# Ten row stores and sixteen stores of encoded weights are issued from ScalarE's queue instead of SyncE's

## The chip, the core and the metric

The kernel runs on one core of a Trainium2 chip. Five engines have an instruction stream each: TensorE (PE, with its weight loads listed as PEld), VectorE (DVE), ScalarE (ACT), GpSimd (POOL) and SyncE (SP). The metric is the device time of one execution in microseconds (us), lower being better. SP issues nearly all transfers of the kernel before; its issues are listed as SPq, those of ScalarE as ACTq.

## The reference

```python
for t in range(S):                       # retention, B=4 H=8 S=768 D=64
    state = gamma * state + einsum('bhd,bhe->bhde', k[:, :, t], v[:, :, t])
    y[:, :, t] = scale * einsum('bhd,bhde->bhe', q[:, :, t], state)
x = y.transpose(0, 2, 1, 3).reshape(B * S, H * D)        # 3072 x 512
h = x @ w_in;  x = maximum(0.01 * h, h) @ w_out          # 512 -> 2048 -> 512
h = x @ w_in2; out = where(h > 0, h, exp(minimum(h, 0)) - 1) @ w_out2
```

The weights come as float64, and the matrix products are made in split fp32 (a high and a low half, three products each).

## The kernel before, in words

**Stages.** The retention is computed in 24 chunks of 128 tokens (six for each of four sequences). A first list schedule, not touched, covers chunks 0 to 13 and the first steps of the first network. A second list schedule covers the rest: chunks 14 to 23 beside the last old-style steps of the first network, then both networks in groups of seven products by a Strassen-like scheme. The order of PE's work is written out; the order on ACT, DVE, POOL and SP comes from a planner. It takes tasks with an engine, a cost, the tasks they depend on and a lag after their end, and places on each engine in turn the one that its model can start first. Every engine's stream is then run in that order.

**A chunk c (14 to 23).** PE makes the scores (`sc`, L262), DVE masks them (`pt`, L317), PE makes the outputs and state (`o`, L271 to L285), ACT copies the output rows out of PSUM into the tile `xs` (task `xs`, L293), and a transfer stores them into the DRAM scratch `xscr` (task `xso`, L289). There is one `xs` tile, so the copy of chunk c+1 waits until the store of chunk c has landed. DVE adds the state (`st`, L299, or L301 for a sequence's first chunk). The scores of the next chunk use the same PSUM bank, so they wait for `xs` and `st`. Between them PE makes a first product (L920) and a second product (L929) of the old-style steps. The rows of `xscr` are read back later for the products (L1187).

**Encoded weights i (0 to 7).** The high and low weights are added on DVE into two tiles `fe` (L1028, twice: tasks `fa` and `fb`), four differences go into a tile `te` (L1029 to L1032), ACT writes the high halves over the two `fe` tiles (`hi0`, `hi1`, L1040), DVE takes the low halves in `te` (L1041), and three transfers go into the DRAM scratch `w1enc`: `sh0` and `sh1` (L1042, from `fe`) and `sl` (L1044, from `te`). The two `fe` tiles are all there are, so the next `fa` and `fb` wait for the landing of `sh0` and `sh1`. The sum `fa` is also the last reader of a piece of the weights, and its end frees the room into which rows of `xscr` are loaded (tile `w`, L1187), which ACT then casts (L1173).

**Groups.** In a group, products 0 to 6 (L1242) go to PSUM banks; ACT copies three of them out (L1268), DVE adds others (L1276), and product 4 needs the second of those copies. The operands of the products are made from loaded rows by DVE (L1170), cast by ACT (L1173) and split by DVE (L1177).

Completion of transfers is counted on eight semaphores that all transfers take in turn, whichever engine issues them, so a transfer also waits for the one that had its semaphore before.

Of the kernel before, what the change touches and what calls it, by code (L numbers as in the profile page):

```python
# [33 lines left out]
C = 128  # L34
# [5 lines left out]
CPB = BLK // C  # L40
# [19 lines left out]
def body(ctx: ExitStack, tc: tile.TileContext, kkv, w1, w2, tabs, rows, out):  # L60
    nc = tc.nc
# [9 lines left out]
    xscr = {j: dp.tile([P, KD, BLK], F32, name=f"xscr{j}") for j in range(2, NB)}  # L71
    w1enc = [dp.tile([P, NPR, BLK], F32, name=f"w1enc{i}") for i in range(HM)]
# [96 lines left out]
    def conv_ops():  # L169
        yield c_put, pieces[0]  # L170
        for n, i in enumerate(pieces):
            yield c_exp, i
            yield c_bias, i
            if n:
                yield c_split, pieces[n - 1]
            yield c_top, i
            yield c_low, i
            yield c_sign, i
            if n + 1 < len(pieces):
                yield c_put, pieces[n + 1]  # L180
            yield c_mul, i
            yield c_cast, i
        yield c_split, pieces[-1]

    queue = list(conv_ops())
# [22 lines left out]
    with ExitStack() as actx:  # L208
# [16 lines left out]
        def prep_k(c):  # L225

            k = kv[c][:, 2, :].rearrange("p (h d) -> p h d", h=H)
            nc.gpsimd.tensor_tensor(k, k, ktab.unsqueeze(2).to_broadcast([P, H, D]), ALU.mult)

        def prep_q(c):  # L230

            nc.gpsimd.tensor_tensor(kv[c][:, 1, :], kv[c][:, 1, :], qtab, ALU.mult)
# [23 lines left out]
        def quarters(c, sc):  # L256

            for i in range(2):
                for x in range(2):
                    for k, r in HEADS:  # L260
                        a = (2 * i + k) * C + x * HC
                        nc.tensor.matmul(sc[half(k), r, cells(i, x)], kv[c][half(r), 0, a : a + HC], kv[c][half(r), 1, a : a + C - x * HC],  # L262
                                         start=True, stop=True, skip_group_check=True)
# [21 lines left out]
                            nc.tensor.matmul(o[p : p + n, k, pair(i)], st[half(r), 2 * k + i, z * n : (z + 1) * n], kv[c][half(r), 1, pair(2 * i + k)],  # L285
                                             start=False, stop=True, skip_group_check=True)

        def rows_out(c, x):
            nc.sync.dma_start(out=xscr[c // CPB][:, :, c % CPB * C : (c % CPB + 1) * C], in_=x)  # L289

        def rows_copy(o, x):
            y = o[:, :, : 2 * C].rearrange("p k (i t) -> p k i t", i=2)
            nc.scalar.copy(x.rearrange("p (k i) t -> p k i t", k=2), y)  # L293

        def state(c, o):
            n = st.rearrange("p (k i) d -> p k (i d)", k=2)
            m = sg.rearrange("p (k i) d -> p k (i d)", k=2)
            if c % NCB:
                nc.vector.tensor_tensor(n, m, o[:, :, 2 * C : 2 * C + 2 * D], ALU.add)  # L299
            else:  # L300
                nc.vector.tensor_copy(n, o[:, :, 2 * C : 2 * C + 2 * D])  # L301
# [4 lines left out]
        def chunk_tasks(c, task, pe_task, x_bank, t, x, needs, takes=None, uses=None, after=None):  # L306


            cb = c % NCB
            late = {"lag": 2.0} if takes else {}  # L310
            takes, uses = takes or {}, uses or {}

            def more(n):
                return dict(([("use", uses[n])] if n in uses else []) + ([("take", takes[n])] if n in takes else []))

            pe_task(("sc", c), 0.95, needs["sc"], lambda: quarters(c, x_bank()), **more("sc"))
            task(("pt", c), "V", 0.96, [("sc", c)] + needs["pt"], lambda: nc.vector.tensor_tensor(t()[:, :, : 2 * TRI], x_bank()[:, :, : 2 * TRI], steps_mask, ALU.mult), **more("pt"))  # L317
            ready = [("pt", c)]
            if cb < NCB - 1:
                task(("pk", c), "G", 1.05, needs["kv"], lambda: prep_k(c), **more("pk"))  # L320
                ready.append(("pk", c))
            if cb:
                task(("pq", c), "G", 1.3, [("sc", c)], lambda: prep_q(c), **more("pq"))
                ready += [("pq", c)] + needs["st"]
            yield
            pe_task(("o", c), 0.98 + (0.5 if cb < NCB - 1 else 0.0) + (0.67 if cb else 0.0), ready, lambda: outputs(c, x_bank(), t()), **more("o"))
            task(("xs", c), "A", 0.6, [("o", c)] + needs["xs"], lambda: rows_copy(x_bank(), x()), **more("xs"))
            task(("xso", c), "Q", 0.8, [("xs", c)], lambda: rows_out(c, x()), **late, **more("xso"))
            if cb < NCB - 1:
                task(("st", c), "V", 0.41, [("o", c)] + needs["sg"], lambda: state(c, x_bank()), **more("st"))  # L330
            if cb < NCB - 2:
                task(("sg", c), "V", 0.55, [("st", c)], lambda: decayed(c), **more("sg"))
# [466 lines left out]
        def task(key, eng, cost, deps, fn, use=(), take=None, lag=0.0):  # L799

            queued.update((key, d[1]) for d in deps if d is not None and d[0] == "queued")
            tasks[key] = eng, cost, [d[1] if d[0] == "queued" else d for d in deps if d is not None], fn, take, lag
            uses_of[key] = list(use) + ([take[1]] if take else [])
            for u in uses_of[key]:
                uses.setdefault(u, []).append(key)
            if eng == "P":
                pe.append(key)
# [93 lines left out]
        for k in range(2):  # L901
            f = lazy(lambda: cv.tile([P, 2, BLK], F32, tag="f", name="nt"))
# [53 lines left out]
        for s in range(N0, NS):  # L956
# [3 lines left out]
                 use=[("gf", s), ("gfs",)], take=("ghi", ("ghi", s)))  # L960
# [47 lines left out]
        def enc_tasks(i):  # L1008
            n = QB
            EA, EB, ET, U = ("ea", i), ("eb", i), ("et", i), ("encs",)  # L1010

            def enc(op, eng, cost, deps, fn, use=(), take=None, lag=0.0):
                task(("e", i, op), eng, cost, [("e", i, d) if isinstance(d, str) else d for d in deps], fn, list(use) + [U], take, lag)

            def whole(m):
                return lambda: (f32(wt[0, m, 0][:, :BLK]), f32(wt[0, m, 0][:, BLK:]))

            def tw(k):
                return at(ET)[:, k]

            def fa():
                return at(EA)

            def fb():
                return at(EB)

            for nm, m, key in (("fa", i, EA), ("fb", i + HM, EB)):
                enc(nm, "V", 0.69, [], lambda w=whole(m), key=key: tt(at(key), *w(), add), use=wa(m), take=("ef", key))  # L1028
            enc("t1", "V", 0.42, ["fa", "fb"], lambda: tt(tw(1), fb()[:, :n], fa()[:, :n], sub), use=[EA, EB], take=("pf", ET))  # L1029
            enc("t3", "V", 0.42, ["t1"], lambda: tt(tw(2), fb()[:, n:], fb()[:, :n], sub), use=[EB, ET])  # L1030
            enc("t2", "V", 0.42, ["t1"], lambda: tt(tw(0), fb()[:, n:], tw(1), sub), use=[EB, ET])
            enc("t4", "V", 0.42, ["t2"], lambda: tt(tw(3), fa()[:, n:], tw(0), sub), use=[EA, ET])  # L1032
            for k, key, before in ((0, EA, ["t2", "t4"]), (1, EB, ["t2", "t3", "t4"])):
                def hi(key=key):
                    return at(key).rearrange("p (b c) -> p b c", b=2)

                def t(k=k):
                    return at(ET)[:, 2 * k : 2 * k + 2]

                enc(f"hi{k}", "A", 0.62, before, lambda hi=hi, t=t: nc.scalar.copy(hi().bitcast(F32R), t()), use=[key, ET])  # L1040
                enc(f"lo{k}", "V", 0.7, [f"hi{k}"], lambda hi=hi, t=t: tt(t().bitcast(F32R), t(), hi(), sub), use=[key, ET])  # L1041
                enc(f"sh{k}", "Q", 0.8, [f"hi{k}"], lambda hi=hi, k=k: nc.sync.dma_start(out=w1enc[i][:, 2 + 2 * k : 4 + 2 * k, :n], in_=hi()),  # L1042
                    use=[key], lag=4.0)
            enc("sl", "Q", 0.9, ["lo0", "lo1"], lambda: nc.sync.dma_start(out=w1enc[i][:, 2:6, n:], in_=at(ET)), use=[ET], lag=4.0)  # L1044
            for k in (0, 1, 6):
                stored["e", i, k] = []
            for k in range(2, 6):
                stored["e", i, k] = [("e", i, f"sh{k // 2 - 1}"), ("e", i, "sl")]
# [130 lines left out]
        for q, (L, j) in enumerate(SBS):  # L1179
# [28 lines left out]
            for n in ("11", "12", "22", "s3", "s1", "s2", "s4"):  # L1208
                if n in loaded_by:
                    raw, known, use, take = raw_x(q, n), [loaded_by[n]], [X(n)], None  # L1210
                    free = [("mk", q, "s1")] if n == "22" else []
                else:
                    raw, key = (r3, T("3")) if n == "s3" else (rs, T("s"))
                    known, use, take = [("mk", q, n)], [key] + ([] if n == "s1" else [X(n)]), ("x", X(n)) if n == "s1" else None
# [240 lines left out]
        while able:  # L1455
            pick = {}
            for x, r in able.items():
# [7 lines left out]
                c = (max(r, free[eng]), begin(x))  # L1465
# [4 lines left out]
            eng, cost, _, fn, take, lag = tasks[x]  # L1470
# [108 lines left out]
```

## Time and profile before

| | us |
|---|---|
| median of 3 runs | 1092.84 (1091.79 to 1094.06) |
| the profiled execution | 1092.51 |
| its span | 1090.6 |
| PE busy in the span | 1075.7 (99%) |
| DVE busy | 821.7 (75%) |
| ACT busy | 669.1 (61%) |

The span runs from the first to the last instruction of the profiled execution; 1.9 us of its time lie around it. PE being busy in 99% of the span means that a change can gain little more than PE's idle time, and that whatever makes PE wait longer shows in full.

### The profile page before, as it was taken

The page shows a single profiled execution, that of the slowest core. Times are in us where ns is not written, and L with a number is a line of the kernel's source. Part 1 is how long each engine was busy: PE and PEld are TensorE (multiplying, and loading weights), DVE is VectorE, ACT ScalarE, POOL GpSimd, SP SyncE. Part 2 cuts the span into 40 slices and gives each one's busy share as a digit, 9 for nine tenths or more (in the row PEclk, how much of TensorE's full clock was granted, in tenths as well). Part 3 has the DMA queues.
Part 4 walks back from the last instruction along what each step waited for, and adds up shares of the span by engine and source line. Part 5 has one row for each costly group of instructions (what it writes and reads, how often), then busy time and mean ns, then how long its engine had stood idle before and what let it go on. Part 6 is the DMA issues. An engine that isn't in the chain of part 4 may idle for free.

```text
span 1090.6 us, 18038 instructions
## 1 busy us (share of the span) xinstructions
PE 1075.7 (99%) x6745; PEld 880.5 (81%) x6745; DVE 821.7 (75%) x1300; ACT 669.1 (61%) x1128; POOL 53.9 (5%) x45
## 2 busy tenths in 40 slices
PE   9999999989999999999999999999999999999998
PEld 6778787767888888888888888888888888888886
DVE  5999987776755776557775669989988889979942
ACT  4675552333655665455654478788888778878831
POOL 4111212220000000000000000000000000000000
PEclk9999999999999999999999999999999999999999
DMA  9975547979888877776877966786676776674473
GB/s 353 393 290 192 204 136 236 338 252 314 275 266 273 263 222 219 236 235 206 296 238 247 322 207 188 263 272 202 203 226 192 259 225 193 201 227 149 122 234 108
DMA packets 115600, 258.40 MB, mean 237 GB/s; under 512 B 10924, under 2 KB 41772, under 8 KB 111160
## 3 DMA queue, kind: packets, MB, share of 16 engines
q1 hardware_dynamic: 115488, 257.14, 72.0%
q8 instruction: 54, 0.88, 0.3%
q14 instruction: 34, 0.28, 0.1%
q10 hardware_dynamic: 24, 0.09, 0.0%
HBM read 200.57 MB, written 56.62 MB: 236 GB/s over the span
## 4 chain that ended last, share of the span: by engine, by line
PE 91%; DMA 4%; DVE 4%; issue 1%; ACT 0%; SPq 0%; DVEq 0%; ACTq 0%
PE y L1354 40%; PE x L1242 15%; PE h L1242 10%; PE px L1242 10%; PE h L199 5%; PE y L609 4%; PE y L929 2%; DMA w1enc<-fe 1%; DMA xscr<-xs 1%; PE px L920 1%; DMA kv<-in_kkv 1%; PE x L262 1%; PE x L271 1%; PE x L285 0%; DMA w<-xscr 0%
## 5 line engine op out<-in xcount | busy, mean ns | idle before, releaser
L1354 PE MATMUL y<-w,ghi 128*128 128x512 f32 x768 | 236.4, 389 | 0.0
L1354 PE MATMUL y<-ghi,w 128*128 128x512 f32 x512 | 177.0, 389 | 0.0
L1354 PEld LDWEIGHTS y<-w,ghi 128*128 128x128 f32 x768 | 144.0, 188 | 30.0 <-ACT gk L943 0.2
L1354 PE MATMUL y<-w,glo 128*128 128x512 f32 x384 | 149.4, 389 | 0.0
L1354 PEld LDWEIGHTS y<-ghi,w 128*128 128x128 f32 x512 | 96.1, 188 | 20.0
L1242 PE MATMUL x<-w 128*128 128x512 f32 x432 | 109.6, 389 | 0.0
L1374 DVE TENSOR_TENSOR glo<-gk,ghi 128x512 fp32r<-128x512 f32 x92 | 63.3, 689 | 49.4 <-ACT ghi L1371 48.7
L1354 PE MATMUL y<-glo,w 128*128 128x512 f32 x256 | 99.6, 389 | 0.0
L1242 PEld LDWEIGHTS x<-w 128*128 128x128 f32 x432 | 81.1, 188 | 16.8
L1371 ACT CAST ghi<-gk 128x512 fp32r<-128x512 f32 x92 | 57.0, 621 | 60.0 <-PE y L1354 57.8
L1276 DVE TENSOR_TENSOR gk<-gk,x 128x512 f32<-128x512 f32 x67 | 45.9, 686 | 51.5 <-PE x L1242 40.0
L1354 PEld LDWEIGHTS y<-w,glo 128*128 128x128 f32 x384 | 72.1, 188 | 15.1
L1323 DVE SCALAR_TENSOR_TENSOR a<-nt,a 128x512 f32<-128x512 f32 x96 | 65.9, 686 | 8.7 <-ACT nt L1319 8.5
L1331 DVE SCALAR_TENSOR_TENSOR nt<-a,nt 128x512 f32<-128x512 f32 x96 | 66.3, 691 | 2.7
L1327 DVE SCALAR_TENSOR_TENSOR nt<-nt 128x512 f32<-128x512 f32 x96 | 65.7, 685 | 0.0
L1311 ACT ACTIVATE nt<-nt 128x512 f32<-128x512 f32 x96 | 60.8, 633 | 2.7 <-DVE gk L1335 0.2
L1315 ACT ACTIVATE a<-nt 128x512 f32<-128x512 f32 x96 | 60.8, 633 | 2.2
L1242 PE MATMUL h<-w 128*128 128x512 f32 x240 | 60.9, 389 | 0.0
L1242 PE MATMUL px<-w 128*128 128x512 f32 x240 | 60.9, 389 | 0.0
L1319 ACT ACTIVATE nt<-nt 128x512 f32<-128x512 f32 x96 | 59.4, 620 | 0.0
L1354 PEld LDWEIGHTS y<-glo,w 128*128 128x128 f32 x256 | 48.0, 188 | 10.0
L199 PE MATMUL h<-xhi,w 128*128 128x512 f32 x168 | 55.3, 394 | 0.0
(205 smaller groups left out, 2048.4 us busy)
## 6 DMA issues: line engine op xcount, KB each, us to landing
w<-w2scr SPq DMA_DIRECT2D x96, 512.0 KB, 4.0
w<-w1scr SPq DMA_DIRECT2D x168, 256.0 KB, 3.4
w<-w1enc SPq DMA_DIRECT2D x112, 256.0 KB, 3.9
kv<-in_kkv SPq DMA_DIRECT2D x22, 1024.0 KB, 7.5
raw<-in_w SPq DMA_DIRECT2D x40, 512.0 KB, 5.3
raw<-in_w SPq DMA_DIRECT2D x12, 1024.0 KB, 9.5
w2scr<-raw SPq DMA_DIRECT2D x16, 512.0 KB, 4.3
w1enc<-w SPq DMA_DIRECT2D x24, 256.0 KB, 3.9
```

The source lines that it names most:

```text
L199: nc.tensor.matmul(h, a, x, start=(n == 0), stop=(n == 3 * KD - 1))
L1242: nc.tensor.matmul(to, a, x, start=(first and z == 0), stop=(z == 5), skip_group_check=True)
L1276: task(("s", *hk[b]), "V", 0.7, [("c", *hk[b])] + deps, lambda: tt(at(t), at(t), bank[name], add), use=[t])
L1311: nc.scalar.activation(t, n, AF.Tanh, scale=-0.5)
L1315: nc.scalar.activation(a, t, AF.Copy, bias=-0.5, scale=0.5)
L1319: nc.scalar.activation(n, n, AF.Exp, scale=-1.0)
L1323: nc.vector.scalar_tensor_tensor(out=a, in0=n, scalar=1.0, in1=a, op0=ALU.add, op1=ALU.mult)
L1327: nc.vector.scalar_tensor_tensor(out=t, in0=n, scalar=1.0, in1=t, op0=ALU.add, op1=ALU.mult)
L1331: nc.vector.scalar_tensor_tensor(out=t, in0=a, scalar=2.0, in1=t, op0=ALU.add, op1=ALU.mult)
L1354: nc.tensor.matmul(ybank[d], a, x, start=(first and n == 0), stop=(last and n == 2))
L1371: task(hi, "A", 0.62, [made_by, last_hi[0]], lambda h=h, hi=hi: nc.scalar.copy(at(hi), at(h)), use=[h], take=("ghi", hi))
L1374: task(lo, "V", 0.7, [hi], lambda h=h, hi=hi, lo=lo: tt(at(lo), at(h), f32(at(hi)), sub), use=[h, hi], take=("glo", lo))
```

## The change

Sixteen stores of `fe` tiles (`sh0`, `sh1` of i = 0 to 7) and the ten stores of rows of chunks 14 to 23 are issued by ACT, from its own queue, where SP issued them. For the planner they become tasks of ACT of 0.5 us each, with lags of 5.0 and 5.5 us (before: 0.8 us of SP, lags of 4.0 and 2.0 us). The order of ACT, DVE and SP in the second list schedule comes out differently everywhere; the order of PE and POOL is the same. The transfers keep their sizes and addresses.

```diff
-        def rows_out(c, x):
-            nc.sync.dma_start(out=xscr[c // CPB][:, :, c % CPB * C : (c % CPB + 1) * C], in_=x)
+        def rows_out(c, x, queue=nc.sync):
+            queue.dma_start(out=xscr[c // CPB][:, :, c % CPB * C : (c % CPB + 1) * C], in_=x)
...
-            late = {"lag": 2.0} if takes else {}
...
-            task(("xso", c), "Q", 0.8, [("xs", c)], lambda: rows_out(c, x()), **late, **more("xso"))
+            if takes:
+                task(("xso", c), "A", 0.5, [("xs", c)], lambda: rows_out(c, x(), nc.scalar), lag=5.5, **more("xso"))
+            else:
+                task(("xso", c), "Q", 0.8, [("xs", c)], lambda: rows_out(c, x()), **more("xso"))
...
-                enc(f"sh{k}", "Q", 0.8, [f"hi{k}"], lambda hi=hi, k=k: nc.sync.dma_start(out=w1enc[i][:, 2 + 2 * k : 4 + 2 * k, :n], in_=hi()),
-                    use=[key], lag=4.0)
+                enc(f"sh{k}", "A", 0.5, [f"hi{k}"], lambda hi=hi, k=k: nc.scalar.dma_start(out=w1enc[i][:, 2 + 2 * k : 4 + 2 * k, :n], in_=hi()),
+                    use=[key], lag=5.0)
```

Three places show what becomes of the order. Line numbers of the changed kernel are one lower (L316) or two higher than those of the kernel before.

ACT at chunk 17 and encoded weights 3, before, each row with the semaphores that it waits for (`xs` is the copied row tile, `gf` and `ghi` belong to the old-style steps):

```order
L293 COPY xs_2011<-x2_1891 128x512 [waits DMAHW5_49,DVE_49,PE_49]
L1040 CAST fe_1895<-te_1907 128x512 [waits DMAHW1_49,DVE_49]
L1040 CAST fe_1901<-te_1907 128x512 [waits DMAHW3_49]
L932 ACTIVATE gf_1931<-px_1890 128x512 [waits PE_49]
L959 CAST ghi_1772<-gf_1931 128x512 [waits Activation_49]
L293 COPY xs_2011<-x2_1891 128x512 [waits DMAHW4_49,DVE_49,PE_49]
```

The same place on ACT after the change:

```order
L293 COPY xs_2011<-x2_1891 128x512 [waits DMAHW5_49,DVE_49,PE_49]
L289 DMA xscr4_84<-xs_2011 512x1x128 [waits DMAHW1_49,Activation_49]
L1042 CAST fe_1895<-te_1907 128x512 [waits DVE_49]
L1042 CAST fe_1901<-te_1907 128x512 [waits DMAHW2_49]
L1044 DMA w1enc3_89<-fe_1895 128x2x256 [waits Activation_49]
L1044 DMA w1enc3_89<-fe_1901 128x2x256 [waits DMAHW4_49,Activation_49]
L934 ACTIVATE gf_1931<-px_1890 128x512 [waits PE_49]
L961 CAST ghi_1772<-gf_1931 128x512 [waits Activation_49]
L293 COPY xs_2011<-x2_1891 128x512 [waits DMAHW1_49,DVE_49,PE_49]
```

The row store stands directly behind its copy and the two stores directly behind their casts; the next activation stands behind all three issues.

DVE between the masks of chunk 18 and the encoded weights 4, before (`y0`, `y1` are sums of the old-style steps, `stg` the state):

```order
L317 TENSOR_TENSOR pt_137<-x2_1891,tab_134 128x2x384
L986 TENSOR_TENSOR ws_2160<-ws_2160,y0_1434 128x512 x2
L986 TENSOR_TENSOR ws_2321<-ws_2321,y1_1445 128x512 x2
L1028 TENSOR_TENSOR fe_1895<-w_846 128x512
L301 COPY stg_133<-x2_1891 128x256
L1028 TENSOR_TENSOR fe_1901<-w_1537 128x512
L1029 TENSOR_TENSOR te_1907<-fe_1901,fe_1895 128x256
```

The same place on DVE after the change:

```order
L316 TENSOR_TENSOR pt_137<-x2_1891,tab_134 128x2x384
L1030 TENSOR_TENSOR fe_1901<-w_846 128x512
L988 TENSOR_TENSOR ws_2155<-ws_2155,y0_1434 128x512 x2
L988 TENSOR_TENSOR ws_2321<-ws_2321,y1_1445 128x512
L301 COPY stg_133<-x2_1891 128x256
L988 TENSOR_TENSOR ws_2321<-ws_2321,y1_1445 128x512
L1030 TENSOR_TENSOR fe_1895<-w_1537 128x512
L1031 TENSOR_TENSOR te_1907<-fe_1895,fe_1901 128x256
```

The first encoding sum now stands ahead of the four sums, and takes the tile `fe_1901`, whose store is the second of the two; one of the four sums has moved behind the state copy. At encoded weights 5 the first encoding sum likewise takes the tile of the second store.

ACT at the first group of products, before (`px` is the bank of products 0, 2, 4 and 5; the cast of `xhi1_120` makes an operand of product 6):

```order
L1268 COPY gk_3022<-px_1890 128x512
L1295 ACTIVATE gk_3022<-gk_3022 128x512
L1268 COPY gk_3022<-px_1890 128x512
L1371 CAST ghi_1868<-gk_3022 128x512
L1173 CAST xhi1_120<-ws_2646 128x1024
L99 COPY e2_3064<-raw2_2992 128x512
L1268 COPY gk_3022<-px_1890 128x512
```

The same place on ACT after the change:

```order
L1270 COPY gf_1931<-px_1890 128x512
L99 COPY e2_3031<-raw2_2973 128x512
L1175 CAST xhi1_120<-ws_2646 128x1024
L1270 COPY gf_2042<-px_1890 128x512
L1297 ACTIVATE gf_1931<-gf_1931 128x512
L1373 CAST ghi_1868<-gf_1931 128x512
L106 ACTIVATE e2_3031<-e2_3031,ebias_118 128x512
L1270 COPY gk_3076<-px_1890 128x512
```

The second copy out of `px`, which releases product 4, has moved from ahead of the cast of `xhi1_120` to behind it.

## Rows read from the trace of the kernel before

**Rows 1.** The page, part 1: busy us, share of the span, instructions.

```profile
PE 1075.7 (99%) x6745; PEld 880.5 (81%) x6745; DVE 821.7 (75%) x1300; ACT 669.1 (61%) x1128; POOL 53.9 (5%) x45
```

**Rows 2.** Stretches: PE, PEld, DVE, ACT, POOL busy, granted clock, DMA share, GB/s.

```profile
230.00:240.00 10.00, 7.10 (x81) 5.48 (x83) 7.56 (x10) 1.22 (x2) 2.74 (x2) 0.83 0.76 247
...
164.00:262.00 98.00, 92.42 (x1450) 71.97 (x1449) 72.19 (x112) 32.36 (x53) 22.40 (x16) 0.98 0.85 279
262.00:1086.00 824.00, 824.00 (x3635) 681.72 (x3633) 609.16 (x990) 542.85 (x933) 0.00 (x0) 1.00 0.71 227
```

**Rows 3.** Timeline of PE, 205 to 262 us: start, duration, work [idle before it].

```profile
208.45 0.50 PE L920 MATMUL h<-xhi,w 128*128 128x512 f32 x1
...
212.33 0.90 PE L262 MATMUL x<-kv 64*64 64x128 f32 x32 [0.86 <-DVE stg L301]
...
216.82 0.90 PE L271 MATMUL x<-pt,kv 64*64 64x128 f32 x32 [0.64 <-DVE pt L317]
...
222.35 0.90 PE L262 MATMUL x<-kv 64*64 64x128 f32 x32 [0.60 <-DVE stg L299]
...
233.97 1.56 PE L262 MATMUL x<-kv 64*64 64x128 f32 x32 [2.90 <-DVE stg L299]
...
253.12 0.90 PE L262 MATMUL x<-kv 64*64 64x128 f32 x32 [0.26 <-DVE stg L299]
...
257.27 0.90 PE L271 MATMUL x<-pt,kv 64*64 64x128 f32 x32 [0.31 <-DVE pt L317]
```

**Rows 4.** The chain that ended last, 160 to 265 us: start, us, what.

```profile
201.64 0.42 DVE te L1032
...
203.22 0.63 ACT fe L1040
...
205.69 5.44 DMA xscr<-xs
...
211.23 0.59 ACT xs L293
...
211.85 0.04 DVE stg L301
...
216.24 3.73 DMA w1enc<-fe
...
220.07 0.70 DVE fe L1028
...
220.79 4.61 DMA w<-xscr
...
226.37 0.62 ACT fe L1040
...
227.01 4.83 DMA w1enc<-fe
```

**Rows 5.** Stores from the tile `fe`, 165 to 262 us: issue ns, then landing.

```profile
L1042 SPq DMA_DIRECT2D w1enc<-fe x16: 359/370/564, 170.5 to 257.5; - x16
...
DMA to landing us min/median/max: 2.1/4.6/5.7
```

**Rows 6.** Stores from the tile `xs`, same stretch.

```profile
L289 SPq DMA_DIRECT2D xscr<-xs x10: 525/525/1510, 175.8 to 261.3; - x10
```

**Rows 7.** Timelines of ACT and DVE, 160 to 262 us.

```profile
202.73 0.59 ACT L293 COPY xs<-x 128x512 f32<-128x512 f32 x1 [5.21 <-DMA xscr<-xs]
...
206.04 2.50 DVE L986 TENSOR_TENSOR ws<-ws,y 128x512 f32<-128x512 f32 x4
```

**Rows 8.** Timelines of SP, DVE and ACT at the first group of products.

```profile
262.57 0.45 SPq L1187 DMA_DIRECT2D xhi<-xscr  x1
...
270.06 1.22 DVE L1170 TENSOR_TENSOR ws<-xhi,ws 128x1024 f32<-128x1024 f32 x1 [1.43 <-DMA xhi<-xscr]
...
271.32 1.05 ACT L1173 CAST xhi<-ws 128x1024 fp32r<-128x1024 f32 x1 [0.98 <-DVE ws L1170]
```

**Rows 9.** Timeline of PE there: product 4, first group.

```profile
271.08 1.52 PE L1242 MATMUL px<-w 128*128 128x512 f32 x6
```

## The prediction

> **What bounds the kernel now.** I read the page first: PE is busy in 1075.7 of the 1090.6 us [rows 1], so only some 15 us can be had at all. Then the stretches: from 262 to 1086 us PE has no idle time, and from 164 to 262 us it is busy in 92.42 of 98 us [rows 2]. The moved stores all lie in that second stretch or end with it, so it alone is at stake, and in it PE misses 5.6 us. PE's timeline says where: six waits, 0.86, 0.64, 0.60, 2.90, 0.26 and 0.31 us, together 5.57 [rows 3]. Each is for DVE, four times for the state of a chunk (stg), twice for a mask (pt). After the wait of 2.90 us the granted clock of the ten us around it is 0.83 [rows 2]; at 0.83 some 1.7 us of work are lost in 10, and PE was at the lower of its two levels (1.2 GHz) for a part of them. All that can be won in the stretch is thus 5.57 + 1.7 = 7.3 us, 0.7%.
>
> DVE is late, but not because it is full: it is busy in 72 of the 98 us [rows 2]. The chain shows why [rows 4]. Its steps from 203 to 232 us are transfers and what they hold up in an engine that runs its stream in order: the store of chunk 17's rows (issued 205.69, 5.44 us), after which ACT may copy the next rows (211.23) and DVE may take the state (211.85); the stores of encoded weights 4 (216.24, 3.73 us), after which DVE can make the next encoding sum (220.07); a load of rows into the room which that sum frees (220.79, 4.61 us); the casts on ACT behind it (226.37); the stores of weights 5 (227.01, 4.83 us). DVE's next sums wait for these, and the state which PE wants at 231.1 stands behind them.
>
> **What the change removes.** The row stores. The cast at 203.22 follows chunk 17's copy on ACT, so that copy was over by then; its store was issued 2.5 us later by SP. Issued by ACT at about 203.3, with the landing that it had (5.44), it lands at 208.8, and since chunk 18's outputs end at 208.45 [rows 3], its copy can run at 208.8 instead of 211.23. The copy of chunk 17 had itself waited 5.21 us, to 202.73, for a store [rows 7]. So the waits of copies for stores shrink to almost nothing. The last two idle times of PE, 0.26 and 0.31, I take as gone with them: 0.57 us, bounds 0 and 0.57.
>
> **What it adds.** Twenty-six issues on ACT: 10 of 0.53 us [rows 6] and 16 of 0.37 us [rows 5], 11.2 us; at the longest rows (1.51 and 0.56) 24 us. ACT is busy in 32.36 of 98 us [rows 2], so both ends are covered as a whole; behind a pair of stores an activation starts about 0.7 us later, and its result is used by a second product a whole chunk later. I cost it at nothing. Were that cover gone, each chunk would lose at most those 0.7 us, and PE 7 us over ten. Each moved store also waits for the transfer that had its semaphore before it, eight places earlier in the common order, and if that one is late ACT stands, with the next activation and the next copy behind it. Below it costs nothing; above, one wait as long as the rest of a landing, at most 5.7 us [rows 5]. I take nothing, since with eight transfers in turn at landings of some 5 us the earlier one has as a rule landed when the ninth is issued.
>
> **What it moves: two rounds through the encoding sums.** Here the order decides. Call L the time from the issue of such a store on ACT to its landing; on SP it was 2.1 to 5.7 us with a median of 4.6 [rows 5].
>
> Round one, weights 3 to 4. The differences of weights 3 end at 202.06, and ACT then was held by the late copy until 203.3 [rows 4, 7]. With the copy early the casts run from 202.1, two of 0.62, and the second store is issued at 203.35. DVE now has the sum that needs that store ahead of three of the four sums and of the state. So the state of chunk 18 starts at 203.35 + L + 0.70 (sum) + 3 x 0.625 (2.50 for four [rows 7]) = 205.93 + L, but not before its copy is done (208.8 + 0.59 = 209.4). Before it stood at 211.85. One further sum (0.625) has moved behind it. The differences of weights 4 thus end 211.85 - 205.93 - L - 0.625 = 5.3 - L earlier, 1.8 at most.
>
> Round two, weights 4 to 5. The stores of weights 4 move forward by 5.3 - L from 216.24. But the next sum now takes the tile of the second store, 0.6 us behind the first: it starts at 216.84 - (5.3 - L) + L = 211.54 + 2L, where it stood at 220.07. From there to the stores of weights 5 it is 6.94 us as before (the load and the casts keep their places), and these then land after L in place of 4.83. PE's scores behind them come earlier by (220.07 - 211.54 - 2L) + (4.83 - L) = 13.36 - 3L. This is the whole effect at 233.97, that of the first three waits of PE included, since PE has caught up with all of them there; it cannot be over 5.0 (their sum with the 2.90).
>
> L = 3.7, the row for just such a store at just that place (3.73 [rows 4]), gives 2.3 us. The ends: 2.1 to 2.5 gives 4.9 to the cap; 5.7 gives -3.7. I take 3.7, because SP will have issued less ahead of the store of 227.01, whose 4.83 is the longer of the chain's two. The wait at 231 us then stays above 2 us, and I leave the loss of clock where it is.
>
> **A new wait at the first group.** Product 4 starts at 271.08 [rows 9] and needs a copy on ACT that now stands behind the cast of xhi. That cast follows a DVE sum which waited for its load until 270.06; the cast itself ran from 271.32 for 1.05 us [rows 8]. The copy (0.6) would end at 273.0, 1.9 us late. All of it is timed from the same last first product of PE, so an earlier PE does not shrink it. The load was issued at 262.57, behind the store of the last rows on SP; without that issue (0.53) it is 1.4 us. Bounds 0 and 1.9, since a landing 1.4 us shorter would hide it.
>
> **Sum.** 2.3 + 0.57 - 1.4 = 1.4 us off the profiled 1092.51, so 1091.1; the median of the runs is 0.33 above that execution, so 1091.4.
>
> **Rivals.**
> B, stores from a queue of their own land sooner, L at 2.5. For it: landings of like stores range from 2.1 to 5.7 us [rows 5], and a store on SP stands in line behind SP's loads, such as that of 220.79 [rows 4], so waiting in line can be part of the 4.6. Against: the transfer engines are the same, and busy in 0.85 of the stretch [rows 2]. Round one is then capped at 1.8, the sum of weights 5 starts at 216.84 - 1.8 + 2.5 = 217.54, and the gain is 2.53 + 2.33 = 4.9; with 0.57 - 1.4 it is 4.0, and 5.7 with the clock kept: 1087.1.
>
> C, they land no sooner than the median, L = 4.6: 13.36 - 13.8 = -0.4, then +0.57 - 1.4: 1.3 us slower, 1094.1, no measurable change. The change then has moved the waits, not removed them, because the second tile and the order eat what the early issue gives.
>
> The Trainium skill, page "DMA: Bandwidth & Descriptors", section "Issuing engines are not separate DMA queues", states that transfers started by different engines run on the same 16 DMA engines, and that issuing from several saves only issue time; by that rule C is the case. Its section "Queues, rings and completion order" states that each of these engines takes turns between the queues, packet by packet, which speaks for B where SP has much in line. No row here shows either, since before the change one queue issued all these stores.
>
> D, slower: the stores on ACT land later than on SP, because the loads that SP can now issue sooner (it no longer stops for ACT's results) move beside them. At L = 5.7, the longest row [rows 5], DVE stands at the sum ahead of the state in both rounds: 13.36 - 17.1 = -3.7, with 0.57 - 1.4 it is 4.6 us slower, 1097.4. It decides from L = 4.9 on.
>
> **Numbers.** About 0.2%, 2.2 us, is what a measurement of this kernel tells from no change. Faster than that needs L under 3.4, slower needs L over 4.9. Chances: 0.38 for the forecast (L about 3.2 to 4.2; its own range 1089.5 to 1093.0), 0.28 for B, 0.17 for C, 0.17 for D. Faster: all of B and 0.14 of the forecast, 0.42. Slower: nearly all of D and 0.03 of C, 0.19. The rest, 0.39, is the same. The range goes from B's time to short of D's, 1087.0 to 1096.0.
>
> **What would show it.** Right: the wait of row copies for their stores gone; the idle of PE at 212 us gone; a wait of about 2.4 us left before the scores that stood at 233.97, ended by DVE behind a sum that waited for a store; an idle time of about 1.4 us ahead of product 4 of the first group. The landing of the stores from ACT gives L directly. Wrong: an activation of the old-style steps that PE waits for (then issues on ACT do cost), a wait of ACT in front of a store, or idle time of PE in the stretch after 300 us, which the new order could bring anywhere and which I have put at nothing.

## The result and the profile after

| | before | after |
|---|---|---|
| median of 18 runs, us | 1092.62 (1091.24 to 1095.91) | 1097.26 (1094.18 to 1106.65) |
| ratio, 95% interval | | 1.0059 (1.0044 to 1.0073) |
| profiled execution, span, us | 1092.51, 1090.6 | 1105.25, 1103.5 |

The change makes the kernel slower by 0.59%, against a forecast of 1.4 us faster, and its runs spread over 12.5 us in place of 4.7. (The ratio counts every run; the medians are 4.6 us apart, the means 6.1.) The profiled execution of after is 8 us above the median, so its waits are longer than those of a typical run. The page and the stretches of after, as in [rows 1, 2]:

```profile
PE 1074.3 (97%) x6745; PEld 879.5 (80%) x6745; DVE 822.2 (75%) x1300; ACT 672.1 (61%) x1128; POOL 52.8 (5%) x45
```

```profile
0.00:164.00 164.00, 156.84 (x1666) 125.24 (x1667) 139.48 (x199) 93.58 (x143) 32.44 (x29) 1.00 0.70 261
164.00:275.00 111.00, 94.37 (x1453) 73.61 (x1452) 74.27 (x114) 34.09 (x54) 20.36 (x16) 0.95 0.82 260
...
240.00:250.00 10.00, 6.11 (x88) 5.03 (x92) 7.04 (x9) 0.00 (x0) 2.74 (x2) 0.66 0.24 85
275.00:1098.00 823.00, 822.07 (x3627) 680.11 (x3626) 607.07 (x987) 543.58 (x930) 0.00 (x0) 1.00 0.72 226
```

PE is idle for 111 - 94.37 = 16.6 us from 164 to 275, where before it was 5.6: 11 us of the loss. Another 7.2 lie ahead of 164 (4.75 before), in a part that the change doesn't touch; they are no part of the loss, since the first scores behind 164 start at 168.59, 0.7 us earlier than in before (169.31). Behind 275 there is 0.9 us. PE's waits in the stretch and the one behind it, as in [rows 3]:

```profile
195.99 0.90 PE L262 MATMUL x<-kv 64*64 64x128 f32 x32 [1.42 <-ACT xs L293]
216.02 1.29 PE L262 MATMUL x<-kv 64*64 64x128 f32 x32 [3.78 <-DVE stg L301]
230.96 0.90 PE L271 MATMUL x<-pt,kv 64*64 64x128 f32 x32 [0.80 <-DVE pt L316]
243.89 1.56 PE L262 MATMUL x<-kv 64*64 64x128 f32 x32 [8.02 <-DVE stg L299]
265.24 0.90 PE L262 MATMUL x<-kv 64*64 64x128 f32 x32 [2.57 <-DVE stg L299]
...
560.24 1.45 PE L1244 MATMUL px<-xlo,w 128*128 128x512 f32 x5 [0.93 <-DVE xlo L1179]
```

Three of the first five are for a state (`stg`), and the one that stood at 233.97 with 2.90 us stands at 243.89 with 8.02. In the ten us around its end (240 to 250) the granted clock is 0.66: after an idle time of 8 us PE ran a part of them at the lower level (1.2 GHz). The chain that ended last, 180 to 250 us, as in [rows 4]:

```profile
183.69 11.58 DMA xscr<-xs
...
195.35 0.59 ACT xs L293
...
204.63 8.42 DMA w1enc<-fe
...
220.92 3.63 DMA w1enc<-fe
...
225.36 5.47 DMA w<-xscr
...
232.97 9.74 DMA w1enc<-fe
...
243.50 0.34 DVE stg L299
```

These are the steps of before, with landings of 8.42, 3.63 and 9.74 us for the stores of weights 3, 4 and 5. (The issue of the last one alone took 1.62 of its 9.74 us.) The stores from `fe`, as in [rows 5] (who waits: us, times):

```profile
L1044 ACTq DMA_DIRECT2D w1enc<-fe x16: 364/367/1621, 169.8 to 266.1; - x16
...
  DVE fe L1030: 21.0, 7
...
DMA to landing us min/median/max: 2.2/5.7/9.7
```

DVE stood 21.0 us, seven times, in front of a sum whose tile's store had not landed; before it was 6.1 us, four times. Of the row copies (idle time of ACT before them, us, times, by what ended it; issue ns; landing):

```profile
L289 ACTq DMA_DIRECT2D xscr<-xs x10: 520/527/591, 175.1 to 271.2; - x10
...
  DMA xscr<-xs: 6.4, 2
  DMA w1enc<-fe: 4.5, 1
...
DMA to landing us min/median/max: 3.0/6.0/11.6
```

In before they waited 17.8 us for such stores, in four times. The issues are short in the median, as costed; the landings of `fe` went from 2.1/4.6/5.7 to 2.2/5.7/9.7. SP's order changed as well. SP in before, around the stores of weights 3:

```profile
203.86 0.89 SPq L1042 DMA_DIRECT2D w1enc<-fe  x2
...
205.69 1.51 SPq L289 DMA_DIRECT2D xscr<-xs  x1
207.29 1.20 SPq L1187 DMA_DIRECT2D w<-xscr  x1
```

And in after, first SP, then ACT with the stores of weights 3 and 5:

```profile
204.25 0.32 SPq L1189 DMA_DIRECT2D w<-xscr  x1
205.80 0.37 SPq L1046 DMA_DIRECT2D w1enc<-te  x1
...
225.78 7.61 SPq L997 DMA_DIRECT2D kv<-in_kkv  x2
```

```profile
202.64 0.52 ACTq L289 DMA_DIRECT2D xscr<-xs  x1
...
204.12 1.30 ACTq L1044 DMA_DIRECT2D w1enc<-fe  x2
...
232.45 2.14 ACTq L1044 DMA_DIRECT2D w1enc<-fe  x2
```

The load of rows (512 KB), which stood 3.4 us behind the stores of weights 3, now runs beside them. The row store of chunk 17 (256 KB), which stood 1.8 us behind them, is now issued 1.5 us ahead of them on the same queue. At weights 5 a second load of 1 MB is issued at the end of the 7.61 us of SP's last row, at 233, together with the store of 232.97.

### The profile page after: what moved, and what is told of

It is laid out like the page before. It is cut to its first block, busy times and chain, and to the rows that moved or that the text cites. A ratio compares the mean times of both kernels' runs of the same rounds, so it can differ in the third digit from the quotient of the medians.

```text
span 1103.5 us, 18044 instructions
## 1 busy us (share of the span) xinstructions
PE 1074.3 (97%) x6745; PEld 879.5 (80%) x6745; DVE 822.2 (75%) x1300; ACT 672.1 (61%) x1128; POOL 52.8 (5%) x45
## 4 chain that ended last, share of the span: by engine, by line
PE 88%; DMA 7%; DVE 3%; ACT 1%; issue 1%; SPq 0%; ACTq 0%; DVEq 0%
PE y L1356 39%; PE x L1244 15%; PE px L1244 10%; PE h L1244 10%; PE h L199 5%; PE y L611 4%; DMA kv<-in_kkv 2%; DMA w1enc<-fe 2%; PE y L931 2%; DMA xscr<-xs 1%; PE x L262 1%; DMA w1enc<-te 1%; PE x L271 1%; PE px L922 1%; DMA w<-xscr 0%
```

## The experiments

**Theories.** Q: a store on ACT's queue lands late because it has to share with SP's loads. O: the new order costs, namely DVE's encoding sum ahead of the state (at chunk 18, and at chunk 20, where before has it too). L: SP, freed of waits for ACT, issues its loads too close together. Each kernel was timed beside before, and its ratio is to the runs of before in the same session, whose median was between 1091.25 and 1092.41 us.

**Queue and order apart.** `order_alone` keeps the planner's new entries and issues all from SP:

```diff
-lambda: rows_out(c, x(), nc.scalar), lag=5.5
+lambda: rows_out(c, x()), lag=5.5
-lambda hi=hi, k=k: nc.scalar.dma_start(out=w1enc...
+lambda hi=hi, k=k: nc.sync.dma_start(out=w1enc...
```

> All entries of the planner as changed, but all 26 stores issued by SP again, so the new order of DVE, ACT and SP without the new queue. Theory Q (a store on ACT's queue lands later beside SP's loads): stores of fe land as they did before, median about 4.6 us, DVE waits for them 6 to 10 us in the stretch, 1092 to 1094 us. Rival O (the new order on DVE, the encoding sum ahead of the four sums and the tile of the second store first, is what costs): PE's waits for the state stay, 10 us or more in all, and the time stays at 1096 to 1098 us.

Measured: 1096.55 us, 1.0051 (1.0032 to 1.0069). DVE's timeline, SP's issues, and the landing of the stores of 200 to 216 us (KB each, median us):

```profile
212.92 0.69 DVE L1030 TENSOR_TENSOR fe<-w 128x512 f32<-128x512 f32 x1 [6.10 <-DMA w1enc<-fe]
...
215.32 0.42 DVE L301 COPY stg<-x 128x256 f32<-128x256 f32 x1
```

```profile
201.99 0.53 SPq L289 DMA_DIRECT2D xscr<-xs  x1
204.26 0.32 SPq L1189 DMA_DIRECT2D w<-xscr  x1
204.68 1.78 SPq L1044 DMA_DIRECT2D w1enc<-fe  x2
```

```profile
w1enc<-fe SPq DMA_DIRECT2D x2, 256.0 KB, 7.4
```

The state stands at 215.32 behind a sum that waited 6.10 us; in before it was at 211.85 [rows 4]. The median landing is 4.3 us, but at this place it is 7.4, on SP too, where before had 4.6: the row store of chunk 17 and the load of rows, which before issues behind these stores, now stand ahead of them in SP's line. (No run moves one of the two alone.) So O holds in the time: the order alone costs 5 us, and a late landing needs no second queue. It does not hold in the waits: PE's waits for states are 7.1 us in all (4.6 in before), short of the 10 that O asked for.

`queue_alone` keeps the order of before on PE, DVE and ACT's computing, and issues each store from ACT directly behind its cast or copy:

```diff
-lambda: rows_copy(x_bank(), x())
+lambda: (rows_copy(x_bank(), x()), rows_out(c, x(), nc.scalar) if takes else None)
-lambda hi=hi, t=t: nc.scalar.copy(hi().bitcast(F32R), t())
+lambda hi=hi, t=t, k=k: (nc.scalar.copy(hi().bitcast(F32R), t()),
+    nc.scalar.dma_start(out=w1enc[i][:, 2 + 2 * k : 4 + 2 * k, :n], in_=hi()))
```

> The order of PE, DVE and ACT's computing as before the change, but each of the 26 stores issued by ACT directly behind its cast or copy. Theory Q: landings of fe rise to a median of 5.5 us or more as in the changed kernel, DVE's wait for them doubles, 1095 to 1098 us. Rival O: 1092.6 us or up to 2 us less, with waits of DVE for fe no longer than the 6.1 us of before. Theory L (SP, freed of waits for ACT, issues its loads earlier and closer together, and these delay any store): as Q in time, so this run does not tell Q from L.

Measured: 1096.24 us, 1.0047 (1.0029 to 1.0065). The medians are 5.4 us for `fe` and 8.2 for `xs` (before: 4.6 and 5.7), DVE waits 13.1 us for `fe` stores, PE 5.87 us for the state at 237.89. So Q (or L) holds too. One row store, issued at 184.82, took 10.58 us; the queues (packets, MB, share of 16 engines) from 184.9 to 189 us, and then from 190 to 194 us with SP's first:

```profile
q1 hardware_dynamic: 453, 1.35, 101.4%
```

```profile
q1 hardware_dynamic: 438, 1.27, 84.0%
q10 hardware_dynamic: 454, 0.23, 19.2%
```

For the first 4 us only SP's queue moved packets, with a store of `te` and a load of kv that SP had issued at 183.37 and 184.25, ahead of the row store. Then the two queues moved nearly the same number of packets, 438 and 454, and very different amounts, 2.9 and 0.5 KB a packet. This second part is what the Trainium skill, page "DMA: Bandwidth & Descriptors", section "Queues, rings and completion order", states (each engine takes turns between queues, packet by packet), and there the trace agrees with 438 against 454. In the first part the trace shows no turns, 453 against none. By that section a packet can hold several descriptors, and the profile's packets need not be the same unit; why ACT's queue moved nothing for 4 us stays open. The prediction had read that rule as speaking for the stores; with small packets against large ones it speaks against them, and the stores also waited for what SP had issued before.

`rows_only` moves the ten row stores alone, `enc_only` the sixteen others alone, each with its entries of the planner. Of the change's diff `rows_only` takes back the second part, `enc_only` the first:

```diff
-enc(f"sh{k}", "A", 0.5, ..., lambda hi=hi, k=k: nc.scalar.dma_start(out=w1enc..., lag=5.0)
+enc(f"sh{k}", "Q", 0.8, ..., lambda hi=hi, k=k: nc.sync.dma_start(out=w1enc..., lag=4.0)
```

```diff
-task(("xso", c), "A", 0.5, [("xs", c)], lambda: rows_out(c, x(), nc.scalar), lag=5.5, **more("xso"))
+task(("xso", c), "Q", 0.8, [("xs", c)], lambda: rows_out(c, x()), **late, **more("xso"))
```

> Only the ten row stores move to ACT (planner's entries for them as changed); the stores of encoded weights stay on SP as before. Theory Q: the row stores land later (median about 6 us, up to 10), which only costs where a copy waits for them; 1092.5 to 1094.5 us. Rival O: no more than 1 us away from before, since the encoding sums keep their rule. If the encoded stores carry the whole loss, this is 1092 to 1093 us.

> Only the sixteen stores of encoded weights move to ACT; the row stores stay on SP as before. Theory Q: fe lands at a median of 5.5 us or more and DVE's waits carry most of the loss, 1095 to 1097 us. Rival O: also 1095 to 1097 us, but with fe landing at the 4.6 us of before. If the row stores carry the loss, 1092 to 1093 us.

Measured: 1094.43 us, 1.0027 (1.0015 to 1.0039), and 1091.70 us, 1.0008 (0.9994 to 1.0023). The encoded stores alone cost nothing that can be told, though their landings are as late (median 5.7 us) as in after; that misses what both theories expected. The row stores alone cost 0.27%, which Q expected and O did not. Both runs also change the order of DVE, so neither moves a queue by itself. In `enc_only` both encoding sums stand ahead of the state of chunk 18 and wait 5.46 us for a store, and PE waits 2.9 us for that state; but the 2.90 us at chunk 20 of before are gone. Such a stall thus costs only what it adds to the stalls that before has already.

**Packet sizes.** The loads of kv in rows of 2 KB in place of 8 KB:

```diff
-nc.sync.dma_start(out=kv[c], in_=kkv[c])
+nc.sync.dma_start(out=kv[c], in_=kkv[c].rearrange("n p d -> p n d"))
-np.stack([feature_major(k), ..., token_major(v)], axis=2)
+np.stack([feature_major(k), ..., token_major(v)], axis=1)
```

> The kernel of queue_alone (order of before, the 26 stores on ACT), with the loads of kv in rows of 2 KB in place of 8 KB (the array in DRAM is laid out in four parts), same bytes, same issues. If a store on ACT's queue lands late because its small packets (512 B and 1 KB) take turns with SP's packets one for one, then landings fall where kv was in flight: fe from a median of 5.4 us to 4.5 or less, xs from 8.2 to 6 or less, the state's wait at the scores of 237.89 from 5.87 to under 3, and the time to 1091 to 1094 us. If it is only that SP issues its loads earlier (bytes in flight, not packets), landings and time stay: 1095.5 to 1097 us.

> The kernel before with the same 2 KB rows in the loads of kv: the control for the run beside it. All stores stand in one line with the loads on SP, so the size of a load's packets should not matter to them: 1090 to 1093 us, landing of fe at a median of 4.3 to 4.9 us, by either theory. If the smaller rows make every transfer slower, this is 1 us or more above before, and the run beside it is to be read against this one.

Measured: 1091.30 us, 1.0003 (0.9985 to 1.0021), and 1093.42 us, 1.0012 (1.0003 to 1.0021). In `queue_2kb`, 164 to 275 us:

```profile
kv<-in_kkv SPq DMA_DIRECT2D x8, 1024.0 KB, 8.1
w1enc<-fe ACTq DMA_DIRECT2D x16, 256.0 KB, 4.5
...
xscr<-xs ACTq DMA_DIRECT2D x10, 256.0 KB, 7.7
```

Against `queue_alone` the loads of kv land 2.0 us later (6.1 there) and the stores of `fe` 0.9 us sooner, and the 0.47% are gone; `xs` came down by 0.5 us only, less than expected. In `queue_2kb` too, a row store issued at 183.30 moved no packet before 187 us. In before, with everything in one line, smaller rows bring no gain (landing of `fe` 4.6, as it was; 1.0 us slower than the 1092.41 of its session). That speaks for packets and against L. But in the changed order it bought nothing:

> The changed kernel with the loads of kv in rows of 2 KB. If the packet sizes of the two queues make the stores late, the part of the loss that is the queue's goes and the part that is the order's stays: fe lands at a median of 4.5 to 5.0 us in place of 5.7, and the time is 1092 to 1096 us. If packets don't matter once the order is as changed, 1097 to 1098 us.

> The kernel of after_state_first (1092.8 us) with the loads of kv in rows of 2 KB. If the packets' part was hidden in the changed kernel by the stall ahead of the state of chunk 18 (there the stores took 9.8 us beside loads that are not kv), it shows now: 1089 to 1091.5 us. If 2 KB rows help only in the order of before, 1092 to 1094 us.

Measured: 1098.24 us, 1.0055 (1.0039 to 1.0072), and 1092.91 us, 1.0021 (1.0001 to 1.0041); the second has the rule of the next but one group added. In `after_2kb` the median of `fe` fell to 4.4 us, and yet the two stores of weights 3, at 200 to 216 us, took longest of all:

```profile
w<-xscr SPq DMA_DIRECT2D x1, 512.0 KB, 8.2
w1enc<-fe ACTq DMA_DIRECT2D x2, 256.0 KB, 9.8
w1enc<-te SPq DMA_DIRECT2D x1, 512.0 KB, 8.9
```

Beside them run the load of rows and the store of `te`, whose rows were left as they are, and the row store of chunk 17 stands ahead of them on ACT's queue. Large packets of kv are thus not needed to delay the store that decides in the changed order; which of the others delays it was not tested.

**Lags.** `before_lag` gives the kernel before the planner's lags of the change; `after_lag8` gives the changed kernel lags of 8.0 us; `lag_queue` is `before_lag` with the stores on ACT, as in `queue_alone`.

```diff
-late = {"lag": 2.0} if takes else {}
+late = {"lag": 5.5} if takes else {}
...
-    use=[key], lag=4.0)
+    use=[key], lag=5.0)
```

and in `after_lag8`:

```diff
-rows_out(c, x(), nc.scalar), lag=5.5
+rows_out(c, x(), nc.scalar), lag=8.0
...
-    use=[key], lag=5.0)
+    use=[key], lag=8.0)
```

> The kernel before, all stores on SP, with only the planner's lags raised to those of the change (row stores 2.0 to 5.5 us, encoded stores 4.0 to 5.0 us). If the new order comes from the lags, it is as slow as order_alone, 1095 to 1097 us. If it comes from the entry as work of ACT, it stays within 1 us of before; a small gain, to 1089 us, is possible, since the lag of 2.0 was shorter than any landing but the shortest.

> The changed kernel with the planner told lags of 8.0 us for both kinds of store in place of 5.0 and 5.5. The encoding sum at chunk 18 then stands behind the state again, and each pair of sums together. If half of the loss is the order (sums ahead of states, made for stores that land in 5 us), the two waits of 3.78 and 8.02 us for states fall below 1 and 4 us, and the time to 1090 to 1094 us. If the late landing costs whatever the order, it stays at 1095 to 1098 us.

> The kernel with the raised lags (before_lag, 1088.4 us), same order of PE, DVE and ACT's computing, and the 26 stores issued by ACT directly behind their casts and copies. In that order DVE waited 1.0 us for encoded stores and no copy waited for a row store, so landings that are 1 to 2.5 us later should cost less than the 5 us they cost in the order of before: 1089 to 1092 us, with fe landing at 4.5 us or more in place of 3.4. If a store on ACT costs by its issue or its late landing whatever the order, 1092 to 1094 us.

Measured: `before_lag` 1088.36 us, 0.9967 (0.9954 to 0.9979); `after_lag8` 1096.87, 1.0043 (1.0026 to 1.0059); `lag_queue` 1094.22, 1.0020 (1.0009 to 1.0031). With the raised lags and SP's one line DVE waits for `fe` stores only twice (its row, 160 to 275 us):

```profile
  DVE fe L1028: 1.0, 2
...
DMA to landing us min/median/max: 2.1/3.4/6.7
```

So the raised lags alone do not make the slow order; they make one that is 4 us faster than before, more than expected. The slow order takes the entry as work of ACT (engine and cost), which was not run with the old lags. With the stores on ACT the same order loses 5.9 us (1094.22 - 1088.36, two sessions in which before had 1092.34 and 1092.41), which is more than expected. Part of it goes through the row stores; `lag_queue`'s chain:

```profile
184.85 7.28 DMA xscr<-xs
...
192.83 10.05 DMA xscr<-xs
...
203.57 7.90 DMA xscr<-xs
```

The copies wait 12.5 us for such stores, none in `before_lag`. Part goes through the encoded stores: DVE waits 12.4 us for them (1.0 in `before_lag`), and PE's longest wait, 3.11 us for a mask, stands behind one of 4.42 us of DVE for such a store. In `after_lag8` PE waits for no state; it waits 2.77, 1.82 and 1.72 us for row copies and 1.85 and 2.43 us for masks instead. A longer lag only moves the stall.

**The state ahead of the sums.** The planner may place the sums of weights 4 and 6 only behind the states of chunks 18 and 20:

```diff
-enc(nm, "V", 0.69, [], ...
+enc(nm, "V", 0.69, [("st", 14 + i)] if i in (4, 6) else [], ...
```

On DVE at chunk 18 this makes of the changed kernel:

```order
-L1030 TENSOR_TENSOR fe<-w 128x512
 L988 TENSOR_TENSOR ws<-ws,y_1434 128x512 x2
-L988 TENSOR_TENSOR ws<-ws,y_1445 128x512
+L988 TENSOR_TENSOR ws<-ws,y_1445 128x512 x2
 L301 COPY stg<-x_1891 128x256
-L988 TENSOR_TENSOR ws<-ws,y_1445 128x512
-L1030 TENSOR_TENSOR fe<-w 128x512
+L1030 TENSOR_TENSOR fe<-w 128x512 x2
```

At chunk 20 the state moves ahead of both sums. ACT's order is unchanged; on SP one store changes its place.

> The changed kernel with one thing more: the planner may place the encoding sums of weights 4 and 6 only behind the state of chunk 18 and of chunk 20. Only DVE's stream differs, at these two places; the 26 stores stay on ACT. If what costs is that a sum which waits for a late store stands ahead of the state that PE needs, the waits of 3.78 us at chunk 18 and 8.02 us at chunk 20 fall below 1.5 and 4 us, with the landings as late as in the changed kernel, and the time to 1091 to 1094 us. If late stores cost wherever the sum stands (they delay all later weights), 1095 to 1098 us.

> The kernel before with the same rule for DVE, all stores on SP. Its wait of 2.90 us for the state of chunk 20 stood behind two sums that waited 3.27 us for a store, so it should fall below 1 us, and the time to 1088 to 1091 us. If it stays at 1092 to 1093 us, the delay only moves to the next sums.

> The kernel of order_alone (all stores on SP, order as changed) with the rule that the sums of weights 4 and 6 come behind the states of chunks 18 and 20. If the order's half is wholly these sums, its wait of 3.54 us for the state of chunk 18 falls below 1.5 us and the time from 1096.5 to 1089 to 1092 us. If the loads that the new order puts ahead of the stores on SP cost by themselves, 1094 to 1097 us.

> The kernel of before_state_first (1089.8 us) with the 26 stores issued by ACT directly behind their casts and copies; PE, DVE and ACT's computing in the same order. If late stores cost only where a sum stands ahead of a state, this is within 1 us of before_state_first, 1089 to 1091 us. If the row copies that wait for late row stores cost too (as the 10.58 us of one in queue_alone), 1092 to 1094 us.

Measured: `after_state_first` 1092.77 us, 1.0000 (0.9990 to 1.0011); `before_state_first` 1089.77, 0.9974 (0.9963 to 0.9984); `order_state_first` 1093.22, 1.0011 (0.9998 to 1.0024); `queue_state_first` 1091.71, 0.9993 (0.9978 to 1.0008). The first two are in the range expected of the rule, the last two fall between the two cases expected. In `after_state_first` the stores of weights 3 land hardly sooner (8.2 us in after):

```profile
w1enc<-fe ACTq DMA_DIRECT2D x2, 256.0 KB, 7.9
```

and PE's waits are these, 4.8 us in all and none for a state (its profiled execution, 1090.52 us, is the shortest of its runs):

```profile
194.82 0.90 PE L262 MATMUL x<-kv 64*64 64x128 f32 x32 [0.74 <-ACT xs L293]
217.38 0.90 PE L271 MATMUL x<-pt,kv 64*64 64x128 f32 x32 [2.52 <-DVE pt L316]
226.90 0.90 PE L271 MATMUL x<-pt,kv 64*64 64x128 f32 x32 [0.80 <-DVE pt L316]
236.36 0.90 PE L271 MATMUL x<-pt,kv 64*64 64x128 f32 x32 [0.75 <-DVE pt L316]
```

All ten kernels by order and queue, as ratios to before:

| order | stores on SP | stores on ACT |
|---|---|---|
| of before | 1 | 1.0047 |
| of before, state first | 0.9974 | 0.9993 |
| of the change | 1.0051 | 1.0059 |
| of the change, state first | 1.0011 | 1.0000 |
| of before, raised lags | 0.9967 | 1.0020 |

The first and third lines: the queue alone costs 0.47%, the order alone 0.51, both together 0.59. Either one is enough for the loss, and taking back only one gives nothing that can be told.

Down the columns: the rule takes 0.40 of the 0.51% off the order alone, all of the 0.59% off the change and 0.54% off the queue alone. But it takes 0.26% off before as well, which has such a stall of its own. A sum that waits for a store ahead of the state is thus a part of the loss: beyond the 0.26%, the rule gives back 0.14, 0.33 and 0.28% of the three. With the rule on both sides the change still costs 0.26% (1.0000 against 0.9974, whose intervals do not meet). Of that, 0.09% is the 0.93 us of PE's wait for `xlo`: it is in the traces of after, `order_alone`, `rows_only`, `after_2kb`, `after_state_first`, `order_state_first` and `after_state_2kb`, at 545 to 560 us, and in no other. The rest is open.

Across: in the orders planned for SP the queue costs 0.47, 0.19 (barely told from noise) and 0.53%; in those planned for ACT it costs 0.08 and -0.11%, which the intervals do not tell from nothing. Why the queue costs in one set of orders and not in the other is open. The row copies' waits in `lag_queue` are a reason that the trace shows; that the other orders are free of it was not tested by itself.

## Why the prediction was wrong

- **What bounds the kernel:** right but for 0.93 us. The loss lies in the stretch that it named, in waits for states above all.
- **Row stores issued early, copies freed:** half right. Copies' waits for stores fell from 17.8 to 10.9 us, not to nothing, and the landing was not "that it had". The store that the prediction moved to 203.3 was issued at 202.64 and let its copy run at 210.75, not at 208.8. Another row store took 11.58 us, its copy ended late and PE waited 1.42 us for it, a wait that before had not. The 0.57 us taken as gain did not come.
- **Issues on ACT at nothing:** right. They took 0.53 and 0.37 us in the median (the longest 1.62, and what held it the trace does not say), and no wait of PE is for an activation.
- **The two rounds: here it failed, in the size of L.** The mechanism is as worked out: DVE stands at the sum ahead of the state, and 13.36 less three landings is the effect at the scores of 233.97. With the three that came, 8.42, 3.63 and 9.74, it is 13.36 - 21.79 = -8.4 us; the scores stand at 243.89, 9.9 later. Of the 1.5 us between, 1.3 are the second store of weights 3, issued at 204.63 and not at 203.35. The forecast put 3.7 in for all three, the row of one of them, and that one was right (3.63). The first and the last were not, since L is no constant of a queue: it goes with what has been issued ahead of the store and what runs beside it. The prediction moved the row store of chunk 17 forward itself and did not count that it then stands ahead of the stores of weights 3; and it looked at the new order of ACT and DVE at that place and not at SP's, where the load of rows had moved from behind these stores to beside them. With both ahead of the stores on SP alone, `order_alone` showed 7.4 us where before had 4.6. A smaller slip is "the load and the casts keep their places": from the sum to the stores of weights 5 it took 7.8 us, not 6.94.
- **How much of this a typical run has:** the 8.42 at weights 3 is matched in shorter executions, 7.4 us in `order_alone` (1098.72 us) and 9.8 in `after_2kb` (1097.40), with waits of PE for the state of chunk 18 of 3.54 and 6.08 us. The 9.74 at weights 5 is not: PE's wait for the state of chunk 20 is 0.77 and 1.15 us there, against 8.02. So the first round is shown to repeat; the second is shown only in an execution 8 us above the median.
- **Rival D** came nearest: slower, by landings longer than on SP before. That its time fits (1097.4 against 1097.26) is in part luck, since it put 5.7 in for all three landings and they were 8.42, 3.63 and 9.74, in an execution of 1105.25. It had 0.17, because landings of such stores above 5.7 us were not in the trace of before; 5.7 was taken for the worst case though nothing bound it. Its reason, stores on ACT beside loads that SP issues sooner, is not needed for the loss: with all stores on SP `order_alone` is as slow.
- **Rival C** and the section "Issuing engines are not separate DMA queues" of the same page of the Trainium skill: by that rule only issue time changes hands. The trace differs: with the order kept, the landings of `fe` went from 4.6 to 5.4 us and of `xs` from 5.7 to 8.2.
- **The new wait at product 4 (1.4 us):** it didn't come. The cast of `xhi` ran at 279.49, its load having landed in time (4.7 us from its issue to the sum, against 7.5 in before, within the bound that the prediction gave), and the copy behind it at 281.00 as soon as product 2 had ended.
- **Nothing behind 300 us:** wrong by one wait of 0.93 us, for `xlo` at 560 us, which the new order brought; it is one of the signs of being wrong that the prediction named.

## What to carry to other kernels

Before crediting a store with the landing time of a row, list what the new order issues ahead of it and beside it on every queue: the same 256 KB took 2.2 to 9.7 us here. In an engine that runs in order, place work that waits for a transfer behind the work that the bound engine waits for; that was worth 0.54 and 0.59% with the stores on ACT, 0.26 and 0.40% with them on SP. The choice of queue was worth up to 0.53% in the orders planned for SP, and nothing that can be told in the others. The two best kernels here, 1088.4 and 1089.8 us, leave all stores on SP and change only a lag or such a rule.

## What was not expected of the hardware

In `queue_alone`, from 190 to 194 us, two queues got about equal numbers of packets (438 and 454), so that the one with packets of 0.5 KB got 15% of the bytes; in the 4 us before, the queue whose store was issued later got none. After PE's idle time of 8.02 us the granted clock of the ten us around its end was 0.66, and the scores behind it took 1.56 us in place of 0.90, so a stall of this size costs more than its length.
